# Layer-norm roots of one block moved to GpSimd, an activation table loaded earlier, and one accumulator moved to another bank

## The chip, the cores and the metric

One core of a Trainium2 chip runs the whole program. The metric is the device time of one execution in microseconds (us). The kernel before takes 202.04 us, the median of three runs (201.89 to 202.27).

## The reference, cut to what matters

```python
x = A_x                                  # 2048 tokens x 512
xn = _layernorm(x, axis=-1)              # (x - mean) / sqrt(var + 1e-5)
return x + _A_ref(xn, A_wqkv, A_wo) + _B_ref(xn, B_w_in, B_w_sp, B_b_sp, B_w_out)
# A: q, k, v = xn @ wqkv; local dilated attention (window 8, step 2, 32 heads); @ wo
# B: z = gelu(xn @ w_in); z2 = _layernorm(z[..., 688:]); (z[..., :688] * (w_sp @ z2 + b_sp)) @ w_out
```

The tokens are cut into 16 tiles of 128, kept as four "blocks" j = 0 to 3 of four tiles (tb = 0 to 3) each. Every tile of x is normalised on VectorE and is then transposed for the matmuls; for most tiles a DMA does that. "Tile 2.3" is block 2's tile with tb = 3. A "root" is 1/sqrt(var + eps), which ScalarE makes with one activation table (the root table) loaded; gelu needs another table. The change touches the stretch from 14 to 26 us, where blocks 2 and 3 are normalised and the projections of block 1 and the first gelu inputs run.

## The kernel before: the parts that matter

```python
ps_mm = ...tile_pool(name="ps_mm", bufs=3, space=PSUM)      # matmul accumulators, three buffers
ps_aux = ...tile_pool(name="ps_aux", bufs=2, space=PSUM)    # auxiliary, two buffers

def ln_root(sl):                    # ScalarE: 1/sqrt(var + eps)
    A.activation(rstd[:, sl], mv[:, sl, 1], ACT.Abs_reciprocal_sqrt, bias=eps_t[:])
def ln_apply(i):                    # VectorE: (x - mean) * rstd
    V.tensor_scalar(xall[:, j, tb, :], ..., mv[:, i, 0:1], rstd[:, i:i + 1], ALU.subtract, ALU.mult)
def tr_dma(i):                      # DMA transpose, issued by SyncE in order
    SP.dma_start_transpose(xnT[:, :, i * P:(i + 1) * P], xall[:, j, tb, :])
...
    for n in range(4): ln_stats(i2[n])          # block 2
    ln_root(slice(2, 7, 4)); ln_root(slice(10, 15, 4))
    for i in i2: ln_apply(i); tr_dma(i)
    for n in range(4): ln_stats(i3[n])          # block 3
    ... # q/k parts 0 to 3 of block 1: matmuls, then casts on ScalarE
    pqs[0] = qk_tile()                          # a ps_mm buffer
    qk_part(pqs[0], 1, 3, 2, 4)                 # last half of k part 3
    ln_root(blk_cols(3))                        # the four roots of block 3
    qk_copy(pqs[0], 1, 3, 2, 4)
    for i in i3: ln_apply(i); tr_dma(i)
# then, from a list of steps:  z1.3 z2.0 p1.1 z2.2 zg1.3 p0.1 zg2.0 q2.2 zg2.2 ...
```

In the list of steps, z*j.tb* is a group of 8 matmuls for one gelu input, zg its gelu on ScalarE, q*j.m* 8 matmuls for a quarter of q and k of a whole block (so it reads all four transposed tiles of that block), and p*g.c* a product on VectorE. Every z and every q needs one of the three ps_mm buffers.

Of the kernel before, what the change touches and what calls it, by code (L numbers as in the profile page):

```python
# [8 lines left out]
F32 = mybir.dt.float32  # L9
ACT = mybir.ActivationFunctionType  # L10
ALU = mybir.AluOpType
# [3 lines left out]
P = 128  # L15
# [23 lines left out]
ORD = [1, 2, 3, 0]  # L39
CHUNKS = (1, 1, 1, 1, 1, 1, 1, 1)  # L40
ORDER = """
z1.3 z2.0 p1.1 z2.2 zg1.3 p0.1 zg2.0 q2.2 zg2.2 p0.3 zs2.2 q2.3 p1.2 qc2.2 p1.3 q2.1 qc2.3 p1.0 z1.0 p0.2
qc2.1 w3 z2.1 p0.0 zg1.0 zs1.0 q2.0 p2.2 zg2.1 a1 z2.3 qc2.0 w2 z1.2 zg2.3 p2.3 halo zs2.0 z3.0 p2.0 zg1.2
z1.1 w0 zg3.0 b1 z0.1 zg1.1 p2.1 zs2.3 X0 a0 zg0.1 z3.2 Xg0 zs1.1 z3.3 a2 zg3.2 z3.1 zs1.2 zg3.3 z0.2 b0 zg3.1
X4 b2 zg0.2 zs3.3 L0 L1 Xg4 q3.1 p3.2 zs3.1 p3.0 Lc0 q3.0 Lc1 p3.1 qc3.1 q3.2 p3.3 qc3.0 zs0.1 a3 z0.3 qc3.2
# [19 lines left out]
def slot_w(s):  # L65
    return 4 * (s // 4) + 3 - s % 4
# [3 lines left out]
def kernel(  # L70
# [14 lines left out]
    A = nc.scalar  # L85
    G = nc.gpsimd
# [7 lines left out]
    sb = ctx.enter_context(tc.tile_pool(name="sb", bufs=1))  # L94
    work = ctx.enter_context(tc.tile_pool(name="work", bufs=3))
    ps_mm = ctx.enter_context(tc.tile_pool(name="ps_mm", bufs=3, space=PSUM))
    ps_aux = ctx.enter_context(tc.tile_pool(name="ps_aux", bufs=2, space=PSUM))
# [41 lines left out]
    z2 = sb.tile([P, NT, FH], BF16, name="z2")  # L139
# [11 lines left out]
    mv = sb.tile([P, NT, 2], F32, name="mv")  # L151
    rstd = sb.tile([P, NT], F32, name="rstd")
# [4 lines left out]
    zvar = sb.tile([P, NT], F32, name="zvar")  # L157
    zrstd = sb.tile([P, NT], F32, name="zrstd")
    eps_t = sb.tile([P, 1], F32, name="eps_t")


    k_casts = [[] for _ in range(4)]
# [30 lines left out]
                    base=0, pattern=[[-1, P]], channel_multiplier=1)  # L193
    V.memset(ks[:, :, 0:HALO], 0.0)
    V.memset(z1u[:, 0:NZ1 - 1, FH:FPAD], 0.0)
    G.memset(rsel[:], 1.0)
    G.affine_select(out=rsel[:], in_=rsel[:], compare_op=ALU.is_ge, fill=0.0,
                    base=0, pattern=[[-4, 32]], channel_multiplier=1)
# [8 lines left out]
    def ln_stats(i, parts=1):  # L207
        j, tb = i % 4, i // 4
        w = D // parts
        for h in range(parts):  # L210
            V.bn_stats(stats[:, i, 6 * h:6 * h + 6], xall[:, j, tb, w * h:w * h + w])  # L211
        ln_agg(i, parts)
# [4 lines left out]
    def ln_agg(i, parts=1):  # L217
        V.bn_aggr(mv[:, i, :], stats[:, i, 0:6 * parts])  # L218

    def ln_root(sl):  # L220
        A.activation(rstd[:, sl], mv[:, sl, 1], ACT.Abs_reciprocal_sqrt, bias=eps_t[:])

    def ln_apply(i):
        j, tb = i % 4, i // 4
        V.tensor_scalar(xall[:, j, tb, :], xall[:, j, tb, :], mv[:, i, 0:1], rstd[:, i:i + 1],  # L225
                        ALU.subtract, ALU.mult)
# [22 lines left out]
    def tr_dma(i):  # L249
        j, tb = i % 4, i // 4  # L250
        SP.dma_start_transpose(xnT[:, :, i * P:(i + 1) * P], xall[:, j, tb, :])
# [10 lines left out]
    table = [None]  # L262
# [46 lines left out]
    def qk_part(pq, j, m, b0, b1, ccs=(0, 1), p0=None, kcs=range(C)):  # L309
        sd, c0 = m // 2, 2 * (m % 2)  # L310
        p0 = b0 if p0 is None else p0
        xv = xnT[:].rearrange("p k (b j t) -> p k b j t", b=TB, j=4)
        for cc in ccs:
            for kc in kcs:
                PE.matmul(pq[:, cc, p0 * P:(p0 + b1 - b0) * P], wqk[:, sd, kc, c0 + cc:D:C],  # L315
                          xv[:, kc, b0:b1, j, :], start=(kc == 0), stop=(kc == C - 1))
# [7 lines left out]
    def qk_copy(pq, j, m, b0=0, b1=TB, p0=None):  # L324
        sd, c0 = m // 2, 2 * (m % 2)
        p0 = b0 if p0 is None else p0
        if sd == 0:
            dst = qs[:, j, c0:c0 + 2, b0 * P:b1 * P].rearrange("p c (b t) -> p c b t", b=b1 - b0)
        else:
            dst = ks[:, c0:c0 + 2, HALO:HALO + S].rearrange("p c (b j t) -> p c b j t", b=TB, j=4)[:, :, b0:b1, j, :]  # L330
        cast = A.copy(dst, pq[:, :, p0 * P:(p0 + b1 - b0) * P].rearrange("p c (b t) -> p c b t", b=b1 - b0))  # L331
        if sd == 1:
            for i in k_reads[j]:
                tc.declare_no_dep(cast.ins, i, reason="other token columns of the same rows")
            k_casts[j].append(cast.ins)

    def qk_tile():
        return ps_mm.tile([P, 2, TBS], F32, name="pq", tag="mm")
# [8 lines left out]
    def prod_c(g, c):  # L347

        o, h = g // 2, g % 2
        j = ORD[o]  # L350
        q3 = qs[:, j, c, :].rearrange("p (b t) -> p b t", b=TB)
        off = HALO - DIL * slot_w(4 * h)
        k3 = ks[:, c, off:off + S].rearrange("p (b j t) -> p b j t", b=TB, j=4)[:, :, j, :]
        k4 = bass.AP(k3.tensor, k3.offset, [list(x) for x in k3.ap[0:2]] + [[DIL, 4], list(k3.ap[2])])
        prod = V.tensor_tensor(pr[g % 3][:, c].rearrange("p w b t -> p b w t"),  # L355
                        q3.unsqueeze(2).broadcast_to([P, TB, 4, P]), k4, ALU.mult)
        for jj in range(4):
            if jj not in (j, (j - 1) % 4):
                for i in k_casts[jj]:
                    tc.declare_no_dep(prod.ins, i, reason="other token columns of the same rows")  # L360
                k_reads[jj].append(prod.ins)
# [213 lines left out]
    def blk(j):  # L575
        return [4 * tb + j for tb in range(TB)]
# [4 lines left out]
    def blk_cols(j):  # L581
        return slice(j, NT, 4)
# [7 lines left out]
    i2, i3 = blk(2), blk(3)  # L590
    warm_up(10)
    for n in range(2):
        ln_stats(t0[n], 2)
        ln_root(col(t0[n]))
# [7 lines left out]
    pqs = [qk_tile() for _ in range(3)]  # L602
    ln_stats(t0[2])
    ln_root(col(t0[2]))
    tr_copy(t0[1], pts[1], 2, 4)
    q_tile(0, (0, 1))
# [6 lines left out]
    pt2 = tr2(t0[2])  # L613
    q_tile(1, (2, 3))
    ln_root(col(t0[3]))
    tr_copy2(t0[2], pt2)
    ln_apply(t0[3])
# [38 lines left out]
        ln_stats(i2[n])  # L656
    ln_root(slice(2, 7, 4))
    ln_root(slice(10, 15, 4))
    for i in i2:
        ln_apply(i)  # L660
        tr_dma(i)
    for n in range(4):
        ln_stats(i3[n])
    pqs = [qk_tile() for _ in range(3)]
    for c in range(3):
        qk_part(pqs[c], 1, c, 0, 2)
    pa3 = ps_aux.tile([P, 2, 2 * P], F32, name="pa3", tag="aux")
    qk_part(pa3, 1, 3, 0, 2)
    qk_copy(pa3, 1, 3, 0, 2)
    for c in range(3):  # L670
        qk_part(pqs[c], 1, c, 2, 4)
        qk_copy(pqs[c], 1, c)
    pqs[0] = qk_tile()
    qk_part(pqs[0], 1, 3, 2, 4)
    ln_root(blk_cols(3))
    qk_copy(pqs[0], 1, 3, 2, 4)
    for i in i3:
        ln_apply(i)
        tr_dma(i)
    SP.dma_start(r_w[:, 4096:6144].rearrange("p (k f) -> p k f", k=C),  # L680
                 A_wqkv[:, 2 * D:3 * D].rearrange("(k p) f -> p k f", p=P))
    SP.dma_start(w_z1[:], B_w_in[:, 0:FH].rearrange("(k p) f -> p k f", p=P))
# [26 lines left out]
    for tok in ORDER.split():  # L709
        name = tok.rstrip("0123456789.")  # L710
# [31 lines left out]
```

## Time and profile before

| | before |
|---|---|
| time, median | 202.04 us |
| span in the profile | 200.5 us |
| TensorE busy | 195.8 us |
| VectorE busy | 184.8 us |
| first matmul of z1.3 to first matmul of q2.2 | 21.50 to 25.46: 3.96 us |
| the same at full rate (24 matmuls, 0.146 us apart) | 3.50 us |

TensorE works almost without a gap, so the time is its work plus its few waits.

### The profile page before, as it was taken

To read this page: it belongs to the slowest core of one execution; us is meant where nothing else is said; L and a number is where in the kernel's file an instruction comes from. 1 tells how busy PE (TensorE), PEld (TensorE's weight loads), DVE (VectorE), ACT (ScalarE), POOL (GpSimd) and SP (SyncE) were. 2 spreads that over 40 slices of the span, in tenths; PEclk is the share of its full clock that TensorE was granted. 3 is DMA by queue.
4 is the path that set the end of the run, shared out by engine and by line. 5 is a ranking of instruction groups with operands and counts; after the bars stand their busy time and mean duration, and the time that the engine had idled before them with its cause. 6 is when DMAs were issued, how large, how long until landed. Compare 5 with 4: busy or idle time off the path is not lost.

```text
span 200.5 us, 4090 instructions
## 1 busy us (share of the span) xinstructions
PE 195.8 (98%) x1687; PEld 124.4 (62%) x1691; DVE 184.8 (92%) x249; ACT 104.1 (52%) x176; POOL 18.5 (9%) x14
## 2 busy tenths in 40 slices
PE   7999999999999999999999999999999999999994
PEld 2969746665566666666656666666544656664562
DVE  5789999999989999999979999999999999999624
ACT  3586897999899986463431523808402230331400
POOL 3000000899500000000000000000000000000000
PEclk9999999999999999999999999999999999999999
DMA  5886689950000096534377999199930278209863
GB/s 157 262 249 162 104 95 272 207 91 3 0 0 3 3 148 106 171 73 104 39 174 164 245 219 181 31 233 172 215 70 0 76 185 195 72 31 128 216 208 105
DMA packets 66562, 25.91 MB, mean 129 GB/s; under 512 B 56496, under 2 KB 66288, under 8 KB 66288
## 3 DMA queue, kind: packets, MB, share of 16 engines
q1 hardware_dynamic: 65824, 25.18, 58.1%
q10 hardware_dynamic: 720, 0.48, 0.8%
q8 instruction: 13, 0.21, 0.4%
q14 instruction: 5, 0.04, 0.1%
HBM read 10.13 MB, written 2.10 MB: 61 GB/s over the span
## 4 chain that ended last, share of the span: by engine, by line
PE 90%; DVE 5%; ACT 3%; issue 1%
PE pg L464 37%; PE pz L257 17%; PE pq L315 7%; PE pv L425 7%; PE po L517 6%; PE po L547 6%; DVE stats L211 3%; PE pwm L586 2%; PE pa L547 2%; PE pq L321 1%; ACT r_qk L331 1%; PE pl L375 1%; DVE r_x L225 1%; DVE mv L218 1%; PE po L526 1%; PE pb L517 1%
## 5 line engine op out<-in xcount | busy, mean ns | idle before, releaser
L464 PE MATMUL pg<-z,r_qk 128*128 128x344 bf16 x448 | 66.8, 309 | 0.0
L464 PEld LDWEIGHTS <-r_qk 128*128 128x128 bf16 x448 | 43.8, 98 | 22.0 <-issue 0.4
L439 DVE TENSOR_TENSOR r_pr<-r_x,r_w 128x2048 bf16<-128x2048 bf16 x32 | 38.4, 1220 | 1.3 <-PE pl L375 1.0
L257 PE MATMUL pz<-w_z,xnT 128*128 128x344 bf16 x256 | 39.3, 309 | 0.0
L443 DVE TENSOR_TENSOR r_pr<-r_pr 128x2048 bf16<-128x2048 bf16 x28 | 33.9, 1220 | 0.4
L257 PEld LDWEIGHTS <-xnT 128*128 128x128 bf16 x256 | 25.0, 98 | 13.2 <-issue 0.4
L470 ACT ACTIVATE gs<-pg,b_col 128x688 bf16<-128x688 f32 x16 | 13.2, 835 | 35.3 <-PE pg L464 26.3
L355 DVE TENSOR_TENSOR r_pr<-r_qk 128x2048 bf16<-128x2048 bf16 x24 | 27.9, 1227 | 0.5 <-ACT r_qk L331 0.5
L315 PE MATMUL pq<-xnT,r_w 128*128 128x512 bf16 (+1 forms) x136 | 24.7, 335 | 0.3 <-ACT z L275 0.3
L315 PEld LDWEIGHTS <-r_w 128*128 128x128 bf16 x144 | 15.8, 114 | 8.1 <-issue 1.0
L684 POOL CAST b_col<-b 128x16 f32<-128x16 bf16 x1 | 16.5, 16468 | 33.3 <-DMA b<-in_B_b_sp_dram 33.3
L530 ACT CAST r_qk<-po 128x512 bf16<-128x512 f32 x10 | 5.5, 589 | 22.7 <-PE po L547 22.7
L331 ACT CAST r_qk<-pq 128x1024 bf16<-128x1024 f32 (+1 forms) x16 | 15.4, 984 | 2.4 <-PE pq L315 2.3
L306 ACT ACTIVATE r_uz<-pz 128x688 bf16<-128x688 f32 x16 | 11.8, 741 | 6.6 <-PE pz L257 6.5
L517 PE MATMUL po<-r_lg,r_pr 32*128 32x512 bf16 x192 | 14.5, 375 | 0.0
L425 PE MATMUL pv<-xnT,r_w 128*32 128x512 bf16 x256 | 14.2, 379 | 0.0
L547 PEld LDWEIGHTS <-r_uz 128*128 128x128 bf16 x85 | 8.0, 98 | 9.5 <-issue 1.1
L364 DVE TENSOR_TENSOR r_pr<-r_pr 128x4096 bf16<-128x4096 bf16 x6 | 13.8, 2296 | 0.0
L547 PE MATMUL po<-r_w,r_uz 128*128 128x512 bf16 x56 | 12.7, 379 | 0.5 <-issue 0.5
L281 ACT ACTIVATE junk<-z 128x688 bf16<-128x688 bf16 x16 | 12.4, 775 | 0.1
L275 ACT ACTIVATE z<-pz 128x688 bf16<-128x688 f32 x16 | 11.8, 741 | 1.2 <-PE pz L257 1.2
L425 PEld LDWEIGHTS <-r_w 128*32 128x32 bf16 x256 | 9.5, 138 | 4.3
(85 smaller groups left out, 196.4 us busy)
## 6 DMA issues: line engine op xcount, KB each, us to landing
r_lg<-in_A_wo_dram SPq DMA_DIRECT2D x8, 256.0 KB, 4.0
r_x<-in_A_x_dram SPq DMA_DIRECT2D x12, 128.0 KB, 3.7
out_dram<-r_qk SPq DMA_DIRECT2D x12, 128.0 KB, 2.1
r_w<-in_A_wqkv_dram SPq DMA_DIRECT2D x8, 128.0 KB, 3.5
r_qk<-in_A_x_dram SPq DMA_DIRECT2D x8, 128.0 KB, 2.3
w_z<-in_B_w_in_dram SPq DMA_DIRECT2D x4, 172.0 KB, 4.1
w_z<-in_B_w_in_dram SPq DMA_DIRECT2D x1, 688.0 KB, 5.5
r_w<-in_B_w_out_dram SPq DMA_DIRECT2D x1, 640.0 KB, 6.6
```

The source lines that it names most:

```text
L257: PE.matmul(pz[:, hh, 0:FHALF], xnT[:, kc, i * P:(i + 1) * P], wz[:, kc, hh * FHALF:(hh + 1) * FHALF], start=(kc == 0), stop=(kc == C - 1))
L315: PE.matmul(pq[:, cc, p0 * P:(p0 + b1 - b0) * P], wqk[:, sd, kc, c0 + cc:D:C], xv[:, kc, b0:b1, j, :], start=(kc == 0), stop=(kc == C - 1))
L331: cast = A.copy(dst, pq[:, :, p0 * P:(p0 + b1 - b0) * P].rearrange("p c (b t) -> p c b t", b=b1 - b0))
L355: prod = V.tensor_tensor(pr[g % 3][:, c].rearrange("p w b t -> p b w t"), q3.unsqueeze(2).broadcast_to([P, TB, 4, P]), k4, ALU.mult)
L364: V.tensor_tensor(pr[g % 3][:, 0:2], pr[g % 3][:, 0:2], pr[g % 3][:, 2:4], ALU.add)
L425: PE.matmul(pv[32 * tb:32 * tb + 32, dd, :], wv[:, kc, 2 * d2 + dd, :], xnT[:, kc, tb * TBS:(tb + 1) * TBS], start=(kc == 0), stop=(kc == ...
L439: V.tensor_tensor(pw_t[n], vp[:, :, off:off + P], a_sb[:, slot_w(w), ts].unsqueeze(1).broadcast_to([P, DH, P]), ALU.mult)
L443: V.tensor_tensor(pw_t[n] if dst is None else dst, pw_t[n], pw_t[m], ALU.add)
L464: PE.matmul(pg[:, hh, 0:FHALF], wsp[n][:, k, :], z2[:, k, hh * FHALF:(hh + 1) * FHALF], start=(k == 0), stop=(k == NT - 1))
L517: PE.matmul(pc, op[32 * tb:32 * tb + 32, d, o * P:(o + 1) * P], wo_r[32 * tb:32 * tb + 32, d, cs], start=(d == 8), stop=False, tile_positi ...
L547: mm = PE.matmul(pc, uT[:, o % 2, m, tb * P:(tb + 1) * P], wout[:, m, cs], start=False, stop=(m == MCH - 3))
L684: G.tensor_copy(b_col[:], b16[:])
```

## The change

The intent is to end ScalarE's stand before the first gelu. The roots of block 3, which keep the root table in place until the statistics of block 3 are done, go to GpSimd (add, then power -0.5), tile by tile. So the gelu table can be loaded behind the roots of block 2, ahead of the casts of block 1. The last half of k part 3 takes an auxiliary bank, so that the three z tiles get the three matmul buffers.

```diff
+    mhalf = sb.tile([P, 1], F32, name="mhalf")
+    G.memset(mhalf[:], -0.5)
+    def ln_root_pool(i):
+        G.tensor_tensor(rstd[:, i:i + 1], mv[:, i, 1:2], eps_t[:], ALU.add)
+        G.tensor_tensor(rstd[:, i:i + 1], rstd[:, i:i + 1], mhalf[:], ALU.pow)
 ...
     ln_root(slice(10, 15, 4))
+    A.preload_act_table_set("gelu_apprx_tanh_and_others")
+    table[0] = "gelu"
     for i in i2: ln_apply(i); tr_dma(i)
-    for n in range(4):
+    for n in range(3):
         ln_stats(i3[n])
+        ln_root_pool(i3[n])
+    ln_apply(i3[0]); tr_dma(i3[0])
+    ln_stats(i3[3]); ln_root_pool(i3[3])
+    for i in i3[1:3]: ln_apply(i); tr_dma(i)
 ...
-    pqs[0] = qk_tile()
-    qk_part(pqs[0], 1, 3, 2, 4)
-    ln_root(blk_cols(3))
-    qk_copy(pqs[0], 1, 3, 2, 4)
-    for i in i3: ln_apply(i); tr_dma(i)
+    pa3 = ps_aux.tile([P, 2, 2 * P], F32, name="pa3", tag="aux")
+    qk_part(pa3, 1, 3, 2, 4, p0=0)
+    qk_copy(pa3, 1, 3, 2, 4, p0=0)
+    prod_c(1, 1)                       # p1.1, taken out of the list of steps
+    ln_apply(i3[3]); tr_dma(i3[3])
```

(Loops are put on one line here.)

More of the change, by code (lines that the diff above doesn't have):

```diff
@@ L41 @@
 ORDER = """
-z1.3 z2.0 p1.1 z2.2 zg1.3 p0.1 zg2.0 q2.2 zg2.2 p0.3 zs2.2 q2.3 p1.2 qc2.2 p1.3 q2.1 qc2.3 p1.0 z1.0 p0.2
+z1.3 z2.0 z2.2 zg1.3 p0.1 zg2.0 q2.2 zg2.2 p0.3 zs2.2 q2.3 p1.2 qc2.2 p1.3 q2.1 qc2.3 p1.0 z1.0 p0.2
 qc2.1 w3 z2.1 p0.0 zg1.0 zs1.0 q2.0 p2.2 zg2.1 a1 z2.3 qc2.0 w2 z1.2 zg2.3 p2.3 halo zs2.0 z3.0 p2.0 zg1.2
@@ L661 @@
         tr_dma(i)
-    for n in range(4):
+    for n in range(3):
         ln_stats(i3[n])
+        ln_root_pool(i3[n])
+    ln_apply(i3[0])
+    tr_dma(i3[0])
+    ln_stats(i3[3])
+    ln_root_pool(i3[3])
+    for i in i3[1:3]:
+        ln_apply(i)
+        tr_dma(i)
     pqs = [qk_tile() for _ in range(3)]
@@ L672 @@
         qk_copy(pqs[c], 1, c)
-    pqs[0] = qk_tile()
-    qk_part(pqs[0], 1, 3, 2, 4)
-    ln_root(blk_cols(3))
-    qk_copy(pqs[0], 1, 3, 2, 4)
-    for i in i3:
-        ln_apply(i)
-        tr_dma(i)
+    pa3 = ps_aux.tile([P, 2, 2 * P], F32, name="pa3", tag="aux")
+    qk_part(pa3, 1, 3, 2, 4, p0=0)
+    qk_copy(pa3, 1, 3, 2, 4, p0=0)
+    prod_c(1, 1)
+    ln_apply(i3[3])
+    tr_dma(i3[3])
     SP.dma_start(r_w[:, 4096:6144].rearrange("p (k f) -> p k f", k=C),
```

## The prediction

> **What bounds the kernel now.** I first read the busy shares, then the chain that ended last, then every wait of TensorE, because only the removal of TensorE idle time can shorten a program that this engine fills.
>
> ```profile
> PE 195.8 (98%) x1687; PEld 124.4 (62%) x1691; DVE 184.8 (92%) x249; ACT 104.1 (52%) x176; POOL 18.5 (9%) x14
> ...
> PE 90%; DVE 5%; ACT 3%; issue 1%
> ```
>
> The first line gives busy time by engine, the second the shares of the chain. TensorE is busy for 195.8 of 200.5 us, VectorE for 92%. The granted clock is at 9 tenths or more in all 40 slices. Next, all the waits of TensorE in the whole execution (who waited on whom, us in total, times, longest):
>
> ```profile
> PE pwm L586 <- DVE warm L189: 1.1, 1, 1.1
> PE po L547 <- issue: 0.5, 3, 0.2
> PE pq L315 <- ACT z L275: 0.3, 1, 0.3
> ```
>
> There are 1.9 us in all. 1.1 us is the start of the program, 0.5 us lies at the output projection, and neither is in the part that the diff edits. The change can reach only the third line. What follows is the timeline around that wait (start, length, engine, line, what; in brackets the idle time before it and its cause):
>
> ```profile
> 21.50 3.66 PE L257 MATMUL pz<-w_z,xnT 128*128 128x344 bf16 x24
> 25.46 0.81 PE L315 MATMUL pq<-xnT,r_w 128*128 128x512 bf16 x3 [0.29 <-ACT z L275]
> ...
> 22.49 0.30 ACT L221 ACTIVATE rstd<-mv,eps_t 128x4 f32<-128x4 f32 x1 [0.56 <-DVE mv L218]
> 22.70 0.57 ACT L331 CAST r_qk<-pq 128x512 bf16<-128x512 f32 x1
> 23.28 1.28 ACT L275 ACT_TABLE_LOAD   x1
> 24.57 0.74 ACT L275 ACTIVATE z<-pz 128x688 bf16<-128x688 f32 x1
> 25.21 0.20 ACT L275 ACTIVATION_READ_ACCUMULATOR z<-pz 128x1 f32 x1
> ...
> 22.83 1.38 DVE L225 TENSOR_SCALAR r_x<-r_x,mv,rstd 128x512 bf16<-128x512 bf16 x4 [0.37 <-ACT rstd L221]
> ```
>
> The story is in four steps. ScalarE waits for VectorE's last statistics, makes the four roots of block 3 (22.49), copies the late half of q/k part 3 (22.70), loads the gelu table (1.28 us), and only then evacuates the first of the three gelu inputs. That gelu frees the matmul accumulator that the next q tile (q2.2) needs: there are three such buffers, and this tile takes the one of z1.3. The accumulator read ends at 25.41 and TensorE goes on at 25.46.
>
> How much is really lost is more than the bracket: 24 matmuls start 21.50, and back-to-back ones of this shape start 0.146 us apart (16 from 30.64 to 32.97). TensorE would be free to issue at 21.50 + 24 x 0.146 = 25.00. The loss is 0.46 us; the bracket's 0.29 leaves out the modelled overlap of the last matmul.
>
> **What the Trainium skill says.** "ScalarE: Activation LUTs", section What ACT_TABLE_LOAD costs, gives about 1283 ns for any set; the trace has 1.28 us. It can be moved, not shortened.
>
> "SBUF — State Buffer", section Who interferes with whom, says that VectorE in a 2-port mode, or with two SBUF inputs while GpSimd reads SBUF, locks GpSimd out for the whole instruction, and that a one-input VectorE instruction outside those modes does not. The trace agrees strikingly:
>
> ```profile
> 35.98 16.47 POOL L684 CAST b_col<-b 128x16 f32<-128x16 bf16 x1 [33.30 <-DMA b<-in_B_b_sp_dram]
> 52.38 0.30 POOL L697 MEMSET r_x<- 32x256 bf16 x1
> ```
>
> A 16-element cast stands open for 16.47 us beside unbroken VectorE tensor_tensor work, and ends when VectorE has its first gap (its instruction at 47.75 ends at 52.39, the next starts at 52.42). So a GpSimd root is quick beside statistics and stuck beside products. The spans on GpSimd are rough, so this is a warning and not a duration.
>
> "GPSIMD Engine Reference", section 2.1 Instruction dispatch, warns of about 6 us at the first call of a freshly loaded kernel. The first cast, affine select and memset here show nothing of the kind apart from the case above; no power has run yet, so this stays a risk.
>
> **The change part by part.**
>
> *Gelu table behind the roots of block 2.* The second root of block 2 runs 17.89 to 18.19. The load then takes 18.2 to 19.5 instead of 23.28 to 24.56. It delays the copy of part 3's first half (0.59 us, now at 18.21) to 19.5, and the three 1024-wide casts, which start about 0.9 us apart, to about 20.0, 20.9 and 21.8, the last ending near 22.8. The second half's copy (0.57 us) ends near 23.3. The four-tile root (0.30 us) is gone from ScalarE. So the first gelu starts near 23.3 instead of 24.57, its accumulator is free near 24.1, and 0.9 us are left until TensorE asks at 25.00.
>
> *Last k part of block 1 in an auxiliary bank.* The three z tiles now take the three matmul buffers left by the three casts (free near 20.9, 21.8, 22.8), and TensorE asks for them at 21.50, 22.67 and 23.83: margins 0.6, 0.9 and 1.0 us. The auxiliary pool has two buffers, used before by the transposes of block 1 long done. No matmul is added or removed.
>
> *Input by DMA.* q2.2 also needs the fourth transposed tile of block 2. The trace's landing records have it complete at 24.87, the third at 23.60. Its issue (22.39) is bound by the queue, at 1.31 us per transpose, and does not move. So TensorE can resume at about 25.0 and hardly earlier: the gain is capped at 0.46 us by the matmuls themselves, with 0.1 us of margin to the transfer.
>
> *Roots on GpSimd.* VectorE's statistics take 0.80 us a tile. The new order on VectorE, with start-to-start times from the rows above: three statistics from 19.04 to 21.46, apply (0.33) of the first tile, fourth statistics to 22.59, two applies to 23.24, product p1.1 to 24.46, then the fourth apply. The first three roots run beside statistics (one input, no lock) and have 0.8 to 1.5 us each. The fourth is asked for at 22.5, just as applies and then a product hold the port; I expect it to run only when VectorE stops at 24.46. Add and power on 128x1: the dependent affine selects of this trace start 0.28 us apart, so my estimate is 0.3 us for each, 0.6 us in all. VectorE resumes at 25.06, applies, and starts p0.1 at 25.4; before it started at 25.26. Removed wait 0.37, new wait about 0.6: VectorE gains nothing and is some 0.1 us late.
>
> *Does that lateness matter?* The first TensorE work on products, at 47.62, uses a sum that VectorE ended at 46.71: 0.87 us of slack after 0.04 of signalling. TensorE comes 0.46 earlier and VectorE 0.1 later: 0.3 us remain. Then VectorE's own idle of 0.53 us at 57.52, waiting on ScalarE's cast of a TensorE result, takes up the lateness. The last apply at 25.1 is ready 2.5 us before its transpose is issued at 27.63.
>
> Sum: -0.46 us on TensorE, +0 elsewhere, nothing else on its path. 202.04 - 0.45 = 201.6.
>
> **The rivals.** (1) *The fourth root, or all of them, is slow.* If a power costs 1 us or more, VectorE waits at two or three applies. The slack says when it shows: above about 1.0 us for the exposed root, TensorE begins to wait at 47.2 and the gain shrinks one for one; at 1.5 us it is gone; with four roots of 1.7 us each VectorE is 2 us late and the time is about 203.2. For it: the port lock and unknown power cost. Against: rows of one element per partition are short on GpSimd elsewhere (0.10 to 0.29 us). A first-call load of 6 us would begin at 19.9 and give up to +4 us, 206, just at 2%; I hold it at a few per cent.
>
> (2) *The transfer takes the wait's place.* If the fourth transpose lands 0.2 us later than now, the gain falls to 0.3: 201.75. Nothing in the diff delays it.
>
> (3) *The gain is given back later*: TensorE, 0.46 us earlier, finds a late VectorE. Slack before a product sum read at 64.71 is about 1.2 us; before the last output projection (189.2, after sums ended at 188.04) 1.1 us. Both exceed 0.46, so I expect no return, but a lost half would be 201.8.
>
> (4) *More than this*: there is no more TensorE idle time to win, so under 201.3 would be noise or a shorter tail.
>
> **Range and chances.** The runs before spread from 201.89 to 202.27, about 0.2 us either way. With the chief estimate 201.6, upward risks 201.8 to 203, and almost none downward, I put 201.3 to 202.3 at eight in ten. Two per cent is 4 us: faster by that needs twice the whole TensorE idle time, so one in a hundred; slower needs the 6 us load fully exposed, two in a hundred.
>
> **What would show it right or wrong.** Right: TensorE's waits lose the line on z; the q2.2 matmuls start within 25.0 to 25.1; one table load for gelu at about 18.2; VectorE shows one wait of about 0.6 us on GpSimd's root near 24.5 and none at the first three applies; the first product reduction starts near 47.2 with no wait; the span is 200.0 to 200.1. Wrong: q2.2 waiting on a transpose or a cast; GpSimd powers above 0.8 us; a TensorE wait on a product sum near 47; a second table load; or a fourth root that gets the port while VectorE works.

## More of the kernel before

Part 3 lists DMA queues: queue and kind, packets, MB, share of the 16 engines' time.

```profile
q1 hardware_dynamic: 65824, 25.18, 58.1%
...
q8 instruction: 13, 0.21, 0.4%
q14 instruction: 5, 0.04, 0.1%
```

The "instruction" rows I read as the engines' own refills of instructions; the padding runs below bear this out for q14. They are 18 packets in all, the 13 of q8 with 16,384 bytes each and the 5 of q14 with 8,192.

## The result

The changed kernel is slightly slower: 202.64 us (202.51 to 202.82, six runs) against 202.00 us (201.86 to 202.42, six runs) for the kernel before on the same chip. The ratio is 1.0029, 95% interval 1.0016 to 1.0042. Here and below a ratio is the mean time of one kernel's fast runs over that of the other's of the same rounds, so it is not quite the ratio of the medians quoted. The change is well within 2%, but the time lies above the predicted range of 201.3 to 202.3.

The waits of TensorE in the changed kernel (who waited on whom, us in total, times, longest):

```profile
PE pwm L592 <- DVE warm L190: 1.0, 1, 1.0
PE pq L321 <- DMA xnT<-r_x: 0.8, 1, 0.8
PE pt L238 <- DVE r_x L231: 0.3, 1, 0.3
```

The wait of q2.2 on the gelu is gone, as planned. In its place q2.2 waits longer than before, now on a transposed tile. The timeline of TensorE:

```profile
21.39 3.66 PE L263 MATMUL pz<-w_z,xnT 128*128 128x344 bf16 x24
25.88 1.46 PE L321 MATMUL pq<-xnT,r_w 128*128 128x512 bf16 x6 [0.82 <-DMA xnT<-r_x]
```

From z1.3 to q2.2 it is 4.49 us, where it was 3.96 and should have become 3.50. That is +0.53 us, about the size of the loss (0.58 us between the means of the six runs). The other engines did what the change meant them to do. ScalarE first, then GpSimd, then VectorE:

```profile
18.09 1.28 ACT L665 ACT_TABLE_LOAD   x1
...
22.58 0.63 ACT L337 CAST r_qk<-pa 128x512 bf16<-128x512 f32 x1
23.05 0.80 ACT L281 ACTIVATE z<-pz 128x688 bf16<-128x688 f32 x1
23.69 0.25 ACT L281 ACTIVATION_READ_ACCUMULATOR z<-pz 128x1 f32 x1
```

```profile
19.91 0.19 POOL L226 TENSOR_TENSOR rstd<-mv,eps_t 128x1 f32<-128x1 f32 x1 [17.22 <-DVE mv L220]
20.18 0.55 POOL L227 TENSOR_TENSOR rstd<-rstd,mhalf 128x1 f32<-128x1 f32 x1
...
22.61 0.27 POOL L226 TENSOR_TENSOR rstd<-mv,eps_t 128x1 f32<-128x1 f32 x1 [0.23 <-DVE mv L220]
22.96 1.74 POOL L227 TENSOR_TENSOR rstd<-rstd,mhalf 128x1 f32<-128x1 f32 x1
```

```profile
23.07 1.22 DVE L361 TENSOR_TENSOR r_pr<-r_qk 128x2048 bf16<-128x2048 bf16 x1
24.73 0.41 DVE L231 TENSOR_SCALAR r_x<-r_x,mv,rstd 128x512 bf16<-128x512 bf16 x1 [0.44 <-POOL rstd L227]
```

The first gelu starts at 23.05, not at 24.57. A root beside statistics takes 0.82 to 0.89 us from the start of its add to the end of its power. The fourth power stays open 1.74 us, until 0.41 us after the product of VectorE ends at 24.29, and VectorE waits 0.44 us for it. None of that is what TensorE waits for. The chain of waits through this window (start, length, what) leads to the transfer:

```profile
21.72 0.52 DVE stats L213
22.23 3.50 DMA xnT<-r_x
25.74 0.14 issue
25.88 1.24 PE pq L321 x5
```

**Why the transfer took 3.50 us.** For each transpose the trace records 16 landings on the semaphore that TensorE waits for. I read them as 16 shares, one for each DMA engine. For five of the eight transposes of blocks 2 and 3 (from the trace's records; no view prints them):

```
                       tile   issued   1st share  15th    16th    issue to last
before                 2.0    18.43    22.01      22.11   22.12   3.69
                       2.1    19.73    22.42      22.57   22.57   2.84
                       2.2    21.09    23.40      23.59   23.60   2.52
                       2.3    22.39    24.70      24.86   24.87   2.48
                       3.2    26.32    30.36      30.46   30.46   4.14
after                  2.0    18.32    20.69      20.82   20.84   2.52
                       2.1    19.62    21.92      22.03   22.04   2.42
                       2.2    20.93    23.22      23.41   23.42   2.49
                       2.3    22.23    24.56      24.72   25.74   3.50   <- q2.2 waits
                       3.2    26.16    30.18      30.27   30.27   4.11
```

An undisturbed transpose takes about 2.5 us. In the changed kernel the fourth of block 2 had 15 shares in by 24.72 and the sixteenth 1.02 us later. In the kernel before, the first of block 2 was as late, though in all 16 shares (the first landed at 22.01), and it had room: z2.0 asked for it at 22.5. What distinguishes the two moments is an instruction refill. The DMA queues in the 0.6 us around it, in the kernel before (20.2 to 20.8) and in the changed one (24.2 to 24.8), show one packet of q14 each:

```profile
q1 hardware_dynamic: 249, 0.06, 46.0%
q14 instruction: 1, 0.01, 3.2%
```

```profile
q1 hardware_dynamic: 30, 0.00, 4.8%
q14 instruction: 1, 0.01, 3.2%
```

The refill of 8,192 bytes starts at 20.37 before and at 24.38 after. In the changed kernel it begins when the data of the fourth transpose is already through and all but two of its 32 small completion writes (4 bytes each) are out. The last two start at 24.69, as the packet of the refill ends (24.38 + 0.31). The transposes of tile 3.2, late in both, have the 16,384-byte refill of q8 beside them (28.04 and 27.85).

The Trainium skill, "DMA: Bandwidth & Descriptors", section Queues, rings and completion order, supplies a mechanism: the semaphore increment that ends a transfer "lands only after every earlier write from that SDMA engine, across its queues". A share behind an 8 KB refill on its engine would be held back while the other 15 are not. The trace agrees with the picture (one share, 1.02 us; two writes that start within 0.01 us of the refill's end), but its records do not name the engine of a packet, so that the refill and the late share were on one engine is inferred. Nor does the refill's own 0.31 us make up the delay: the late share landed 1.05 us after its writes started, where 0.37 us is usual (24.50 to 24.87 in the kernel before), and no record shows why.

This gives theory F: *the refill, moved by 4 us, fell on the transpose that q2.2 needs.* The rivals were that the refill falls anywhere and one profile was chance (L), that the loss comes from VectorE's new order and its wait for the fourth root (V), and, for what moved the refill, a change in the number of GpSimd instructions (G) or VectorE's order and waits (O).

### The profile page after: what moved, and what is told of

Same layout as the page of the kernel before. It is cut to its first block, busy times and chain, and to the rows that moved or that the text cites. A ratio compares the mean times of both kernels' runs of the same rounds, so it can differ in the third digit from the quotient of the medians.

```text
span 200.9 us, 4102 instructions
## 1 busy us (share of the span) xinstructions
PE 195.9 (97%) x1691; PEld 123.9 (62%) x1691; DVE 184.8 (92%) x249; ACT 103.9 (52%) x175; POOL 22.5 (11%) x23
## 4 chain that ended last, share of the span: by engine, by line
PE 87%; DVE 6%; DMA 3%; ACT 2%; issue 0%; SPq 0%
PE pg L470 37%; PE pz L263 17%; PE pq L321 7%; PE pv L431 7%; PE po L553 7%; PE po L523 6%; DVE stats L213 3%; PE pa L553 2%; DMA xnT<-r_x 2%; DMA r_x<-in_A_x_dram 1%; DVE r_x L231 1%; PE pq L327 1%; PE pl L381 1%; ACT r_qk L337 1%; DVE mv L220 1%; PE po L532 1%
## 5 line engine op out<-in xcount | busy, mean ns | idle before, releaser
L321 PE MATMUL pq<-xnT,r_w 128*128 128x512 bf16 (+1 forms) x128 | 23.8, 339 | 0.8 <-DMA xnT<-r_x 0.8
L337 ACT CAST r_qk<-pq 128x1024 bf16<-128x1024 f32 x15 | 14.9, 1015 | 3.4 <-PE pq L321 3.3
L553 PE MATMUL po<-r_w,r_uz 128*128 128x512 bf16 x60 | 13.6, 380 | 0.0
```

The costliest lines, as they stand in the source:

```text
L321: PE.matmul(pq[:, cc, p0 * P:(p0 + b1 - b0) * P], wqk[:, sd, kc, c0 + cc:D:C], xv[:, kc, b0:b1, j, :], start=(kc == 0), stop=(kc == C - 1))
L337: cast = A.copy(dst, pq[:, :, p0 * P:(p0 + b1 - b0) * P].rearrange("p c (b t) -> p c b t", b=b1 - b0))
L553: mm = PE.matmul(pc, uT[:, o % 2, m, tb * P:(tb + 1) * P], wout[:, m, cs], start=False, stop=(m == MCH - 3))
```

## The experiments

Twelve runs, all correct, on top of the changed kernel ("after") or the kernel before. The first four ran together, then the next four, then the last four.

### The changed kernel again

No edit.

> The changed kernel once more, unchanged. Theory F (an 8 KB instruction refill sits on one of the 16 DMA engines beside the fourth transpose of block 2, and that engine's share lands about 1 us after the other fifteen): the refill is found within 0.5 us of 24.4 us again, fifteen shares of the fourth transpose land by about 24.8 and the sixteenth near 25.7, q2.2 starts near 25.9, and the time is 0.5 to 0.7 us above the kernel before. Rival L (the refill falls anywhere, and the one profile was chance): the refill is elsewhere, q2.2 starts at 25.0 in this profile, and the six times spread over 1 us.

Measured: 202.79 against 201.89 us, ratio 1.0045 (1.0018 to 1.0072), four runs from 202.47 to 203.52. The refill is at 25.22, in an execution that started about 0.6 us later throughout (z1.3 at 22.03). Fifteen shares of tile 2.3 land by 25.32, the sixteenth at 26.58. q2.2 waits 1.0 us, and z1.3 to q2.2 is 4.69 us. By the clock the refill is 0.8 us later, outside the 0.5 us expected; counted from z1.3 it is where it was (3.19 us after it, 2.99 in the first profile), so rival L falls.

### The GpSimd roots alone

```diff
 # after, minus the early table load, and with the old bank
-    A.preload_act_table_set("gelu_apprx_tanh_and_others")
-    table[0] = "gelu"
-    pa3 = ps_aux.tile([P, 2, 2 * P], F32, name="pa3", tag="aux")
-    qk_part(pa3, 1, 3, 2, 4, p0=0)
-    qk_copy(pa3, 1, 3, 2, 4, p0=0)
+    pqs[0] = qk_tile()
+    qk_part(pqs[0], 1, 3, 2, 4)
+    qk_copy(pqs[0], 1, 3, 2, 4)
```

> The GpSimd roots and VectorE's new order alone; the gelu table loads where it did in the kernel before (behind the casts of block 1) and the last k part takes a matmul bank. By ScalarE's and TensorE's rows alone q2.2 could start at 25.0 here too, since the copy of part 3 no longer waits for the four roots and the first gelu runs near 23.8. Theory F with the refill moved by the nine added GpSimd instructions: the refill lies near 24.4 as in the changed kernel, q2.2 starts near 25.9, time +0.5 to +0.7 us. Rival (the refill moves because of ScalarE's earlier table load): the refill stays near 20.4, q2.2 starts at 25.0 to 25.1, time -0.3 to -0.5 us.

Measured: ratio 1.0027 (1.0008 to 1.0046). Refill at 24.45, last share of tile 2.3 at 25.81 with the others in by 24.96, z1.3 to q2.2 4.31 us. The part with the roots brings both the displaced refill and the loss; the early table load is not needed for either.

### The auxiliary bank alone

```diff
 # before
-    pqs[0] = qk_tile()
-    qk_part(pqs[0], 1, 3, 2, 4)
+    pa3 = ps_aux.tile([P, 2, 2 * P], F32, name="pa3", tag="aux")
+    qk_part(pa3, 1, 3, 2, 4, p0=0)
     ln_root(blk_cols(3))
-    qk_copy(pqs[0], 1, 3, 2, 4)
+    qk_copy(pa3, 1, 3, 2, 4, p0=0)
```

> The last k part of block 1 in an auxiliary bank, all else as before. Every theory: q2.2 now needs the buffer of z1.3 as before, and the gelu of z1.3 still ends near 25.4, so the time is that of the kernel before within 0.1 us; the refill stays near 20.4 unless it moves at random (rival L), in which case q2.2 may start later.

Measured: ratio 1.0000 (0.9978 to 1.0022), refill at 20.34, z1.3 to q2.2 3.83 us, still waiting on the gelu. As every theory had it.

### Work put in front of the late transfer

```diff
 # after, list of steps
-... zg2.0 q2.2 zg2.2 p0.3 zs2.2 q2.3 ... qc2.1 w3 z2.1 p0.0 ... p2.2 zg2.1 a1 ...
+... zg2.0 z2.1 q2.2 zg2.2 p0.3 zg2.1 zs2.2 q2.3 ... qc2.1 w3 p0.0 ... p2.2 a1 ...
```

> The changed kernel with the tile z2.1 (8 matmuls, 1.17 us, its input landed near 22.0) moved ahead of q2.2, so that TensorE has work until 26.17 and asks for the fourth transpose only then. Theory F: the refill stays near 24.4 and the sixteenth share near 25.7, but nothing waits for it; q2.2 starts near 26.1 without a wait; time -0.3 to -0.5 us against the kernel before. Rival V (the loss comes from VectorE's wait for the fourth root or the later apply): the time stays +0.5 to +0.7 us. If the wait only moves to another tile, the profile names it.

Measured: 201.54 against 201.89 us, ratio 0.9981 (0.9962 to 1.0000). The refill is at 24.66 and the sixteenth share of tile 2.3 at 26.01, as late as ever, but q2.2 now asks only at 26.3 and follows the 32 matmuls of four z tiles after 4.67 us, which is 32 x 0.146: no wait. VectorE's wait of 0.44 us for the fourth root is still there. Rival V falls: with the same roots, order and wait on VectorE, the loss is gone and the predicted gain is there.

### Nine idle GpSimd instructions in the kernel before

```diff
 # before
+    for n in range(9):
+        G.memset(scr[:, n:n + 1], 0.0)
     G.memset(mask[:], 0.0)
```

> The kernel before with nine one-element memsets more at the start of GpSimd, which is idle there; nothing else differs. Theory G (the refill moves with the number of GpSimd instructions): the refill moves from 20.4 to near 24.4, the fourth transpose's sixteenth share lands near 25.7 instead of 24.9, q2.2 starts near 25.9 instead of 25.46, time +0.3 to +0.6 us, although no engine has more to do where it matters. Rival O (the refill moves with VectorE's new order and its wait for GpSimd): the refill stays near 20.4 and the time is that of the kernel before within 0.1 us.

Measured: ratio 1.0007 (0.9992 to 1.0021), refill at 20.23, tile 2.3 whole at 24.84. Theory G falls.

### Nine more in the changed kernel

The same edit in the changed kernel.

> The changed kernel with nine memsets more on GpSimd at the start. Theory G: the refill moves again, by several us, away from the fourth transpose (to 28 or later, or to before 22), q2.2 starts at 25.0 to 25.1 and the time falls to 0.3 to 0.5 us below the kernel before. Rival O: the refill stays at 24.4 to 25.2, q2.2 near 25.9, time +0.5 to +0.8 us.

Measured: ratio 1.0039 (1.0024 to 1.0053), refill at 24.69, last share at 26.05 with the rest in by 25.05, z1.3 to q2.2 4.45 us. G falls here too.

### Ten more instructions on VectorE

```diff
 # after
     V.memset(z1u[:, 0:NZ1 - 1, FH:FPAD], 0.0)
+    for n in range(10):
+        V.memset(scr[:, n:n + 1], 0.0)
```

> The changed kernel with ten one-element memsets more on VectorE in its idle time before the first statistics. If the refill is VectorE's own, it comes ten instructions sooner, near 20.5, and q2.2 starts at 25.0 to 25.1 (time -0.3 to -0.5 us). If it is another engine's, it stays at 24.4 to 25.2 and the time at +0.5 to +0.8 us.

The time was missed, the place of the refill half hit. It moved, by 7.5 us, to 16.88, so it is VectorE's own. There it met another transpose that TensorE needs at once, the last one of block 1: 3.49 us from issue to last landing, where it takes 2.45 us in the kernel before. (All sixteen of its shares were late, not one; so the picture of a single held-back share is not the whole of it.) Timeline of TensorE in this run:

```profile
18.57 2.81 PE L324 MATMUL pq<-xnT,r_w 128*128 128x256 bf16 x24 [0.44 <-DMA xnT<-r_x]
21.22 1.04 PE L324 MATMUL pa<-xnT,r_w 128*128 128x256 bf16 x8
22.10 3.66 PE L266 MATMUL pz<-w_z,xnT 128*128 128x344 bf16 x24
25.60 1.67 PE L324 MATMUL pq<-xnT,r_w 128*128 128x512 bf16 x7
```

The wait on a transposed tile has moved to 18.57, and q2.2 follows z1.3 after 3.50 us without any wait. The gain at q2.2 and the new loss are nearly equal in this profile; the time is 1.0018 of the kernel before (1.0003 to 1.0033), some 0.3 us more than the two explain, and that rest is not accounted for.

### Four more instructions on ScalarE

```diff
 # after
     pts = [tr(t0[n]) for n in range(2)]
+    for n in range(4):
+        A.copy(scr[:, n:n + 1], eps_t[:])
```

> The changed kernel with four one-element copies more on ScalarE in an idle stretch near 5.3. If the refill is ScalarE's own, it comes four instructions sooner (some 2 to 3 us: 21.5 to 22.5) and q2.2 starts at 25.0 to 25.2 (time -0.2 to -0.5 us). If it is another engine's, it stays at 24.4 to 25.2 and the time at +0.5 to +0.8 us.

Measured: ratio 1.0034 (1.0018 to 1.0051). The first refill stays at 24.37; the last share lands at 25.73 with the rest in by 24.57. The second small refill of the execution moved from 34.71 to 26.94, which suggests that this one is ScalarE's (weak evidence: it lies at 28.72 to 35.09 in the other runs on the changed kernel, and at 30.66 in the one with three fewer on VectorE). A lesson in reading: in this run the profile puts the wait of q2.2 down to ScalarE.

```profile
25.87 1.46 PE L322 MATMUL pq<-xnT,r_w 128*128 128x512 bf16 x6 [0.93 <-ACT z L282]
```

q2.2 starts 0.14 us after the last share of tile 2.3, exactly the distance of the chain in the changed kernel (25.74 to 25.88). Where a wait is for several things, the name in the bracket is a guess; here the landing record decides.

### Five more instructions on VectorE

The same edit as with ten, with `range(5)`.

> The changed kernel with five one-element memsets more on VectorE (ten brought the refill from 24.4 to 16.9, onto the fourth transpose of block 1, whose sixteenth share then came 1.1 us late). Theory F: with five the refill lies between the two, at 18 to 22; the fourth transpose of block 2 lands whole by about 25.0, q2.2 follows the first matmul of z1.3 by 3.50 us (24 x 0.146) and waits for nothing, and the time is 0.3 to 0.5 us below the kernel before. If the refill comes onto the first transpose of block 2 that one is 1 us late, which z2.0 has room for. Rival V (something else in the new order costs the time): the time stays 0.4 to 0.8 us above.

Measured: 201.83 against 202.17 us, ratio 0.9981 (0.9966 to 0.9996). The refill is at 19.30, tile 2.3 lands whole at 25.11, and q2.2 follows z1.3 after 3.51 us:

```profile
21.74 3.66 PE L266 MATMUL pz<-w_z,xnT 128*128 128x344 bf16 x24
25.25 2.11 PE L324 MATMUL pq<-xnT,r_w 128*128 128x512 bf16 x9
```

So the changed kernel with five instructions that do nothing added is faster than the kernel before, while without them it is slower. VectorE's wait of 0.4 us for the fourth root is still there. The ratio fell from 1.0029 to 0.9981, or 0.97 us; the distance to q2.2 fell by 0.98 us in the profiles. Within the noise the wait for the late transpose accounts for the whole difference.

### Three fewer instructions on VectorE

```diff
 # after: three memsets go from VectorE to GpSimd
-    V.memset(eps_t[:], EPS)
-    V.memset(ks[:, :, 0:HALO], 0.0)
-    V.memset(z1u[:, 0:NZ1 - 1, FH:FPAD], 0.0)
+    G.memset(...)   # the same three
```

> The changed kernel with three memsets moved from VectorE to GpSimd at the start, so three instructions fewer on VectorE. Theory F: the refill comes later than 24.4, at 25.5 to 28.5, beside a transpose of block 3, which nothing wants before 40 us; q2.2 follows z1.3 by 3.50 us, time 0.3 to 0.5 us below the kernel before. If the refill stays at 24.4 (it comes at a fixed place, not at a count), q2.2 waits as in the changed kernel and the time is 0.4 to 0.8 us above.

Neither branch of the expectation fits, and the time was missed: the refill did not come later in VectorE's work, and q2.2 did not wait all the same. Counted from z1.3 the refill did not move: it starts at 25.12, 3.03 us after z1.3 (2.99 and 3.19 in the two profiles of the changed kernel), with 56 of VectorE's instructions begun, just the three fewer than 59. It starts while the fourth transpose is open (issued 22.90, whole at 25.37), and yet that one took 2.47 us. All 32 of its completion writes had started by 25.00, 0.12 us before the refill; in the changed kernel two had not. So this run escaped by a near miss, and it shows that being open at the refill's start is not enough. The next transpose, tile 3.0, took 4.49 us, with a 16,384-byte refill at 26.63 beside it as well, and nobody waited for it. q2.2 follows z1.3 after 3.50 us. But the edit had a price of its own at the start: the root table, which no wait held up in the kernel before, is now loaded behind the wait for the first statistics, at 4.11 us (probably since the first root now needs GpSimd's memset as well; not tested):

```profile
4.11 1.28 ACT L223 ACT_TABLE_LOAD   x1 [4.11 <-DVE mv L220]
```

In the kernel before that load starts at 2.68 and the root at 4.12; here the root starts at 5.40, and TensorE waits 0.7 us for the first tile. The ratio is 1.0018 (0.9997 to 1.0040).

### VectorE's new order with the roots on ScalarE

The edit is long. VectorE's instructions and their order are those of the changed kernel, with table and bank as before; each `ln_root_pool(i)` becomes `ln_root(col(i))`, placed behind a cast of block 1 on ScalarE.

> VectorE's new order with the roots of block 3 on ScalarE tile by tile, behind the casts, and no GpSimd roots; table and banks as in the kernel before. It asks what moved the refill. If the new order on VectorE did, the refill is near 24.4 and the sixteenth share lands near 25.7. If the waits for GpSimd did, the refill is near 20.4 and the transpose lands whole by 25.0. The time is not the question: ScalarE's four roots and the table load come before the first gelu, so q2.2 starts at 25.5 or later in either case.

Measured: refill at 20.00, tile 2.3 whole at 25.00, z1.3 to q2.2 4.14 us behind the gelu, ratio 1.0013 (0.9989 to 1.0036) from two runs. VectorE's new order does not move the refill; the roots on GpSimd do (24.45 in the run with them alone, at the same table and bank). That it is VectorE's waits for GpSimd is not shown: in the changed kernel the first apply that waits for a GpSimd root starts at 21.34, about 1 us after the time at which the refill came in the kernel before.

### The reordered version again

No edit to the version with z2.1 in front.

> The version with z2.1 ahead of q2.2 once more, unchanged, with five rounds for a narrower interval: 0.3 to 0.5 us (0.15 to 0.25%) below the kernel before, interval below 1; the refill at 24.4 to 25.2, the sixteenth share 1 us behind, no wait of TensorE on a transpose.

Measured: 201.60 against 202.17 us, six runs from 201.41 to 202.00, ratio 0.9977 (0.9961 to 0.9992). The refill is at 24.11 and the last share at 25.47; z1.3 to q2.2 is 4.67 us, without a wait. This version is ahead of the kernel before in two separate calls (the first interval just reaches 1), and 1.25 us ahead of the changed kernel in the call that had both (201.54 against 202.79).

### All runs side by side

"Refill" is the start of the first 8,192-byte refill after 12 us; "2.3" the fourth transpose of block 2 from issue to last landing; the distance is that of z1.3 to q2.2, less 3.50 (for the two reordered runs less 4.67).

| kernel | refill at | 2.3 took | lost before q2.2 | ratio |
|---|---|---|---|---|
| before | 20.37 | 2.48 | 0.46 (gelu) | 1 |
| bank alone | 20.34 | 2.47 | 0.33 (gelu) | 1.0000 |
| before, 9 more on GpSimd | 20.23 | 2.48 | 0.33 (gelu) | 1.0007 |
| order alone, roots on ScalarE | 20.00 | 2.48 | 0.64 (gelu) | 1.0013 |
| after | 24.38 | 3.50 | 0.99 (transpose) | 1.0029 |
| after, again | 25.22 | 3.73 | 1.19 (transpose) | 1.0045 |
| GpSimd roots alone | 24.45 | 3.35 | 0.81 (transpose) | 1.0027 |
| after, 9 more on GpSimd | 24.69 | 3.50 | 0.95 (transpose) | 1.0039 |
| after, 4 more on ScalarE | 24.37 | 3.63 | 1.10 (transpose) | 1.0034 |
| after, 10 more on VectorE | 16.88 | 2.48 | 0.00 (0.44 on an earlier transpose) | 1.0018 |
| after, 3 fewer on VectorE | 25.12 | 2.47 | 0.00 (0.7 at the start) | 1.0018 |
| after, 5 more on VectorE | 19.30 | 2.47 | 0.01 | 0.9981 |
| z2.1 in front | 24.66 | 3.50 | 0.00 | 0.9981 |
| z2.1 in front, again | 24.11 | 3.52 | 0.00 | 0.9977 |

The third column has two values: 3.35 to 3.73 where the refill starts at 24.1 to 25.2 before the transpose's last two completion writes, and 2.47 to 2.48 elsewhere, the run with three fewer on VectorE included. In all seven runs of the first kind one share is late and those two writes start within 0.01 us of the end of the refill.

The traces hold more of the pattern than fits the table. Where the first small refill started 1.64 to 1.94 us after the issue of a transpose, all 16 shares were late (five runs, 3.47 to 3.69 us); at 1.99 to 2.37 us it was one share (the seven), or none (three fewer on VectorE, 2.22); at 0.63 us the cost was only 0.3 us (tile 2.0 with five more on VectorE, 2.80 us). The 16,384-byte refill of q8 does the same to a tile nobody waits for: in five runs it started 1.88 to 2.10 us after the issue of tile 3.1, and that tile's sixteenth share came 1.65 to 2.26 us after the fifteenth.

Two builds led nowhere (nothing here shows it): the power did not compile on VectorE, so the roots could not simply go there, and plain no-operations were dropped by the compiler, which is why the padding is made of memsets.

## Why the prediction was wrong

- *What bounds the kernel, and the 0.46 us to be won*: right. Wherever neither gelu nor transfer is in the way, q2.2 follows z1.3 after 3.50 us, and the whole kernel is then 0.2% faster (201.5 to 201.8), as predicted for the change itself (201.6).
- *The early table load*: right. Predicted 18.2 to 19.5 and a first gelu near 23.3; measured 18.09 to 19.37 and 23.05. The accumulator of z1.3 was free at 23.94 (predicted 24.1), well before 25.0.
- *The bank*: right. No z tile waited for a buffer; alone the part is worth nothing.
- *The roots on GpSimd*: right in kind. Three were done in time; the fourth was exposed for 0.44 us (predicted 0.6). The nearness is partly luck: a power took 0.55 us where 0.3 was estimated (the upper of its "0.10 to 0.29 us" for one-element rows was a 128x128 instruction), but only the power was held up; the add, at 22.61, ran beside VectorE's applies, against the prediction. p0.1 started at 25.06, against 25.26 before and 25.4 predicted, so VectorE was not late at all, and no product sum kept TensorE waiting.
- *The input by DMA*: here the prediction failed. It said that the fourth transposed tile, complete at 24.87, "does not move", with "0.1 us of margin to the transfer", and of the rival in which the transfer takes the wait's place, "Nothing in the diff delays it". The issue hardly moved (22.23 against 22.39). The landing did, to 25.74, since VectorE's instruction refill came 4 us later and fell on it. That took the 0.46 us that the change won and about 0.5 us more. The margin of 0.1 us was not there either: where q2.2 waits for this transpose it starts 0.14 us after the last landing (five runs), and 24.87 + 0.14 is 25.01.

The warning was in the profile of before: the first transpose of block 2 took 3.69 us from issue to landing, the fourth 2.48, and nothing in the prediction asked why. A margin of 0.1 us says little when a transfer of the same kind has just taken 1.2 us longer. The instruction queue was on the page as well, at 0.1% of the DMA time, and was passed over for its size.

What is shown: that the refill is VectorE's (five or ten of its own instructions move it, nine of GpSimd's and four of ScalarE's do not), that a transpose which has run for 1.6 to 2.4 us at its start, with completion writes still to come, lands 0.9 to 1.3 us later, that q2.2 waits for exactly this, and that the loss goes away when either the refill (five more on VectorE) or q2.2 (z2.1 in front) is moved. What stays open is why roots on GpSimd move the refill. When it started, 49 of VectorE's recorded instructions had begun in the kernel before and in the version with the same order and ScalarE roots, but 59 in the changed kernel. In all eight runs with GpSimd roots and nothing added on VectorE, the refill starts within 0.3 us of the end of p1.1 (24.29 in the changed kernel), about when VectorE runs out of work before the fourth root. That is a coincidence worth following up; no run here says by what rule the refill is timed. Nor is the DMA engine of the refill known. And in two of the seven runs it starts 2.27 and 2.37 us after the issue, when the held writes were already due (2.12 us at the latest in undisturbed runs), so something held them before the packet's recorded start.

## What to carry to other kernels

When a wait is removed, look at the landing times of every input that the freed instruction needs, and at how much the same kind of transfer varies in the profile of before; a margin below that variation is a coin toss. Before blaming a schedule for a loss of a few tenths of a us, compare where the instruction refills fall. Work whose inputs landed long ago, put in front of the work whose input is just landing, is the sturdier cure: it helped with the refill in its bad place, while padding instructions only moved the refill, once onto another transfer. Its gain here is small: 0.2%, with one of its two intervals just reaching 1.

## What the Trainium skill lacked or had wrong

- "Runtime: NRT & Kernel Launch", section Instruction fetch mechanics, has refills in blocks of 16 KiB, on the sequencer's own DMA queue, with a cost "mostly hidden". The queue is there in the trace, but only q8 shows 16,384-byte packets (13); VectorE, and as it seems ScalarE, are refilled with 8,192 bytes. And the cost is not always hidden: the refill beside the fourth transpose made TensorE wait 0.8 us, and moving it away took the ratio from 1.0029 to 0.9981, 0.5% of the kernel.
- "DMA: Bandwidth & Descriptors", section Queues, rings and completion order, says that an engine's increment lands only after its earlier writes. No page says that an instruction refill delays a DMA transpose in flight: 3.35 to 3.73 us instead of 2.47 to 2.48 with an 8 KB refill, and 4.11 us for tile 3.2 in the changed kernel, with a 16 KB one.
- The pages consulted give no duration for a power on GpSimd. On 128x1 it took 0.55 us (an add 0.19 to 0.27) beside VectorE statistics, and stayed open 1.74 us beside a product. The 6 us load that "GPSIMD Engine Reference", section 2.1, gives for the first call to a freshly loaded kernel is not in this profile: the first power took 0.55 us like the next two. Whether anything was freshly loaded in the profiled execution is not shown, so this does not speak against the page.
- "SBUF — State Buffer", section Who interferes with whom, has the later of two contending instructions fully blocked. The stuck power agrees in kind: it ended 0.41 us after the product, though its recorded start (22.96) lies before the product's (23.07), and spans on GpSimd are rough. The add at 22.61 took 0.27 us while VectorE ran two applies from 22.45 to 23.16; if these applies were in a 2-port mode, which no row here tells, it should have been blocked too.
